# Retention attention into a routed mixture of experts on one core: token rows renumbered by step, row and sequence, and the first two experts' weights loaded in halves instead of quarters

## The chip, the cores and the metric

One core of a Trainium2 chip runs the whole program. The metric is the device time of one execution in microseconds (us). It was taken in 3 runs of the kernel before: 432.28, 426.81 and 423.11 us, with a median of 426.81 us. A separate execution was recorded by the hardware profiler; every statement about where time goes comes from that one.

## The reference

The computation has two parts. The first is a decayed linear attention over 4 sequences of 768 tokens with 8 heads of 64; its output is 3072 tokens of 512 features. The second sends each token to one of 4 groups by the largest of four logits, then to one of 4 experts in the group in the same way, and computes that expert's two-layer network.

```python
state = gamma[None, :, None, None] * state + np.einsum('bhd,bhe->bhde', k[:, :, t], v[:, :, t])
y[:, :, t] = scale * np.einsum('bhd,bhde->bhe', q[:, :, t], state)
...
x = np.ascontiguousarray(attn_out.transpose(0, 2, 1, 3)).reshape(B * S, H * D)
...
h = np.maximum(xg[mask_e] @ w1[g, e], 0.0)
ye = h @ w2[g, e]
combined = g_w[mask_g][mask_e] * e_w[mask_e]
out[tok_idx] = combined[:, None] * ye
```

So there are 16 experts, each with w1 of 512x1024 and w2 of 1024x512 in 32-bit floats (2 MB each).

## The kernel before

**Attention stage.** The tokens are cut into chunks of 128. A step handles the same chunk of two sequences, so there are 12 steps (`NS2`): steps 0 to 5 for sequences 0 and 1, steps 6 to 11 for sequences 2 and 3. In `attention`, each step `i` computes masked scores (L227, masked on VectorE at L239), the product with the running state (L278), the product with the values (L291), the new state (L253), the routing logits (L310) and, for the step before it, the transpose of the attention result to one row per token (`trans_mm`, L322 and L326). ScalarE copies these rows to the tile `xr` (L329), which has one buffer, and SyncE writes them to the DRAM tensor `xd` (L332). Each step gives 256 rows of 512 floats.

**Loads beside it.** SyncE issues all transfers of this stage from one queue in program order: q, k and v of coming steps (`load`, L177), transposed keys for two steps (`kk`, L204), the write of `xd` and the weights of the first two experts. These two, `ua` (expert 0) and `va` (expert 1), are known in advance, so their weights are fetched during attention by `wload_part` (L604). An expert's weights are four tiles `wf` of 128x2048 floats (two of w1, two of w2). Steps 2 to 9 load two parts of `ua` each; steps 9, 10 and 11 load parts of `va` by the table `NEXT`; the last tile of `va` follows after step 11. Each SyncE transfer uses one of eight completion semaphores in turn, so its issue waits for the transfer eight places before it in the queue.

**Splitting weights.** A 32-bit weight is used as a 16-bit high part `wh` (ScalarE, L616) and a 16-bit rest `wl` (L618). For `ua` GpSimd computes `wl` in pieces of 128x512, at the steps after the load; for `va` VectorE computes it in pieces of 128x1024.

**Routing and lists.** Every second step, `route` finds each token's expert, its slot in that expert's list and its weight, on VectorE. `enlist` (L440) then writes for each token its row number and weight to its slot of the DRAM tensor `meta`, by an indirect transfer that GpSimd issues. The row numbers come from the tiles `src`, filled by `iota` (L142) during setup. After 12 chunks the lists of experts 0 and 1 so far are read back to the tiles `mt` (`listed`, L630), and `gather` (L640, GpSimd, indirect) fetches these tokens' rows of `xd` into `xg`. The second lists of both experts, `ub` and `vb`, are read and gathered after all 24 chunks.

**Expert stage.** TensorE transposes gathered rows (`tpx`, L658), computes the first layer (`hps`, L681) and the second (`yps`, L713, L732, L759, L761), and GpSimd writes each result row to its place in `out` by an indirect transfer (L814). Experts 2 to 15 follow in an order found by list length, with weights in transfers of 1 MB (L590). `general` handles whatever is left in long lists, a loop that usually runs no turn.

**Order.** `manual_schedule` holds each engine to the order in which the code is written; the helper functions `beside`, `extra` and `early` inside `run` put the weight work into the steps.

Of the kernel before, what the change touches and what calls it, by code (L numbers as in the profile page):

```python
# [21 lines left out]
B, H, S, D = 4, 8, 768, 64  # L22
P = 128
NC = S // P
NCH = B * NC
NT = B * S
DM = H * D
# [66 lines left out]


KX = (4, 6)
NEXT = {9: (0, 4), 10: (4, 8), 11: (8, 12)}
KEYED = (9, 10)


class Kernel:
# [13 lines left out]
    def setup(self):  # L115
        nc, cp = self.nc, self.cp
        self.ones = cp.tile([P, P], BF16, name="ones")
        nc.vector.memset(self.ones, 1.0)
        self.cst = cst = cp.tile([P, C_END], F32, name="cst")
        self.load("q", 0, (0,))  # L120
        self.load("k", 0, (0,))
        nc.sync.dma_start(cst, self.a_cst)
        act = cp.tile([P, 1], F32, name="act")
        nc.scalar.activation(act, self.ones[:, 0:1], AF.Copy)
        self.ident = cp.tile([P, P], F32, name="ident")
        make_identity(nc, self.ident)

        self.sh = [self.pp.tile([P, 512], F32, name=f"sh{i}", tag="big", bufs=3) for i in range(3)]
        self.sh.append(self.pp.tile([P, 512], F32, name="sh3", tag="tra", bufs=1))
        for sh in self.sh:  # L130
            nc.vector.memset(sh, 0.0)
        self.wr = cp.tile([P, 4, 32], F32, name="wr")
        nc.vector.memset(self.wr, 0.0)
        self.gx = cp.tile([P, NC, 4, P], F32, name="gx")
        self.stri = cp.tile([P, P], BF16, name="stri")
        nc.vector.tensor_copy(self.stri, cst[:, C_STRI:C_STRI + P])
        self.src = []
        for i, (c0, n) in enumerate(BATCHES):
            self.src.append(cp.tile([P, BM, 2], I32, name=f"src{i}"))
            g, c = divmod(c0 // 2, NC)  # L140
            o = self.src[i][:, :, 0].rearrange("p (c b) -> p c b", b=2)
            nc.gpsimd.iota(o, pattern=[[P, n // 2], [S, 2]], base=2 * g * S + c * P, channel_multiplier=1)  # L142
        self.oh = cp.tile([P, BM + 1, NX], BF16, name="oh")
        nc.vector.memset(self.oh[:, BM, :], 0.0)
        self.base = cst[:, C_SEG:C_SEG + NX]
        warm = self.pp.tile([P, 512], F32, name="warm", tag="log", bufs=1)
        one = self.one = nc.const_aps.tensor(1.0, [P, 512], BF16)
        for i in range(WARM):
            nc.tensor.matmul(warm, one[:, 0:P], one, start=True, stop=True)
        self.log = self.pp.tile([P, 512], F32, name="log", tag="log", bufs=1)  # L150
        n = NP * CAP * 2 // P
        self.fill = cp.tile([P, n // 5], I32, name="fill")
        nc.gpsimd.memset(self.fill, OOB)
        self.meta = self.dp.tile([NP, CAP, 2], I32, name="meta")
        self.metaf = self.meta.rearrange("e r c -> (e r) c")
        self.xd = self.dp.tile([NT, DM], F32, name="xd")
# [160 lines left out]
    def trans_mm(self, i):  # L317

        nc, s = self.nc, self.st[i]
        for u in range(2):  # L320
            for j in range(4):
                nc.tensor.transpose(self.sh[2 + u][:, j * P:j * P + P], s["xt"][:, j, u], self.ident)  # L322
        for u in range(2):
            a = LG + 20 * (i % 2 * 2 + u)
            lg = self.log[:, a:a + 20]
            nc.tensor.matmul(lg, s["ls"][:, u * P:u * P + P], self.cst[:, C_SEL:C_SEL + 20], start=True, stop=True)  # L326
        xr = self.wp.tile([P, 2, DM], F32, name="xr", bufs=1)
        for u in range(2):
            nc.scalar.activation(xr[:, u], self.sh[2 + u], AF.Copy)  # L329
        g, c = divmod(i, NC)  # L330
        xd = self.xd.rearrange("(b r) f -> r b f", r=S)[c * P:c * P + P, 2 * g:2 * g + 2, :]
        nc.sync.dma_start(xd, xr)  # L332


    def route(self, i):
# [259 lines left out]

    def wload_part(self, u, k):

        i, h = divmod(k, 4)
        if k == 0:
            u["wf"], u["wh"], u["wl"] = [None] * 4, [None] * 4, [None] * 4  # L600
        if h == 0:
            u["wf"][i] = self.wst.tile([P, 2048], F32, name="wf", tag="wf", bufs=4)
        cs = slice(h * 512, h * 512 + 512)
        self.nc.sync.dma_start(u["wf"][i][:, cs], (self.a_w1, self.a_w2)[i // 2][u["e"], i % 2][:, cs])  # L604

    def wsplit(self, u, k, n=8, eng=None, high=True, low=True):
# [365 lines left out]
    def run(self):  # L972
        tc, nc = self.tc, self.nc
        with ExitStack() as ctx:
# [29 lines left out]
            def early(i, k, high):  # L1004
                if 0 <= i - 3 < 8:
                    self.wsplit(ua, 2 * i - 6 + k, 16, nc.gpsimd, high=high, low=not high)
# [8 lines left out]
            def beside(i, place):  # L1015

                last = i == NS2 - 1
                if place == -1 and i == 10:
                    self.gather(ua)
                    self.gather(va)  # L1020
                if i == 9 and place == 1:
                    assert self.done >= EARLY
                    self.listed(ua, "early0")
                    self.listed(va, "early1")
                if place == 0:
                    if 2 <= i <= 9:
                        for k in range(2):
                            self.wload_part(ua, 2 * i - 4 + k)
                    for k in range(*NEXT.get(i, (0,))):
                        self.wload_part(va, k)  # L1030
                    if i == 10:
                        self.wsplit(va, 0, low=False)
                        self.wsplit(va, 1, low=False)
                    if last:
                        self.wsplit(va, 0, high=False)
                if place == 2:
                    if last:
                        self.xtrans(ua, 'big', (0,))
                        self.wsplit(va, 2, low=False)
                if place == 1:  # L1040
                    early(i - 1, 0, False)
                    if last:
                        self.wsplit(va, 3, low=False)

            self.wp = pool("wp", 2)
            with ExitStack() as actx:
                apool = lambda name, bufs: actx.enter_context(tc.tile_pool(name=name, bufs=bufs))
                self.lp, self.vp = apool("lp", 1), apool("vp", 1)
                self.attention(extra, beside)
# [9 lines left out]
                self.wsplit(va, k, high=False)  # L1059
            first(2)  # L1060
            self.trans_mm(last)
            for k in range(12, 16):
                self.wload_part(va, k)
            while self.todo:
                self.enlist(*self.todo.pop(0))
# [136 lines left out]
```

## Time and profile before

| What | Value |
|---|---|
| median of 3 runs | 426.81 us |
| profiled execution, its own time | 427.34 us |
| its span, first to last instruction | 425.6 us |
| TensorE (PE) busy | 404.0 us, 95% |
| VectorE (DVE) busy | 290.1 us, 68% |
| ScalarE (ACT) busy | 222.8 us, 52% |
| GpSimd (POOL) busy | 175.9 us, 41% |
| mean granted TensorE clock | 0.992 |
| moved by the 16 DMA engines | 107.94 MB, mean 254 GB/s |

The profile lists instructions by engine, source line, and tile (`out<-in`). PE is the matrix product, PEld the loading of its weights. SP is SyncE; SPq and POOLq are the queues on which these engines issue transfers. A duration is in us unless it says ns; in square brackets behind an instruction stands how long its engine was idle before it and what it was released by. A stretch table gives per stretch the span's window, then each engine's busy time, the granted clock, the busy share of the 16 DMA engines and the rate in GB/s. A wait table gives who waited for whom, total time, number of times and the longest time.

### The profile page before, as it was taken

The page shows a single profiled execution, that of the slowest core. Times are in us where ns is not written, and L with a number is a line of the kernel's source. Part 1 is how long each engine was busy: PE and PEld are TensorE (multiplying, and loading weights), DVE is VectorE, ACT ScalarE, POOL GpSimd, SP SyncE. Part 2 cuts the span into 40 slices and gives each one's busy share as a digit, 9 for nine tenths or more (in the row PEclk, how much of TensorE's full clock was granted, in tenths as well). Part 3 has the DMA queues.
Part 4 walks back from the last instruction along what each step waited for, and adds up shares of the span by engine and source line. Part 5 has one row for each costly group of instructions (what it writes and reads, how often), then busy time and mean ns, then how long its engine had stood idle before and what let it go on. Part 6 is the DMA issues. An engine that isn't in the chain of part 4 may idle for free.

```text
span 425.6 us, 13495 instructions
## 1 busy us (share of the span) xinstructions
PE 404.0 (95%) x5692; PEld 332.4 (78%) x5721; DVE 290.1 (68%) x473; ACT 222.8 (52%) x342; POOL 175.9 (41%) x153
## 2 busy tenths in 40 slices
PE   8899999999798999999999999999999999999991
PEld 4789888787675768585979788897978878879791
DVE  4455585578892557776889786867768777787620
ACT  2135336446541556646556665665766657667520
POOL 4445669748877022340508142351513405222001
PEclk9999999999999999999999999999999999999996
DMA  8999999997536867776776786978788797896001
GB/s 282 378 313 327 373 306 339 336 285 243 161 94 236 333 220 249 245 258 235 257 246 214 259 277 239 315 246 283 266 286 284 272 306 270 280 327 233 27 9 34
DMA packets 36913, 107.94 MB, mean 254 GB/s; under 512 B 13784, under 2 KB 13784, under 8 KB 29684
## 3 DMA queue, kind: packets, MB, share of 16 engines
q1 hardware_dynamic: 25908, 89.76, 61.9%
q0 software_dynamic: 10944, 17.31, 11.7%
q8 instruction: 45, 0.74, 0.7%
q14 instruction: 16, 0.13, 0.1%
HBM read 94.65 MB, written 13.77 MB: 255 GB/s over the span
## 4 chain that ended last, share of the span: by engine, by line
PE 58%; issue 26%; POOL 6%; DMA 4%; DVE 2%; SPq 1%; ACT 0%; POOLq 0%; DVEq 0%; ACTq 0%
PE hps L681 19%; PE yps L713 8%; PE yps L759 6%; PE yps L761 5%; PE op L291 5%; POOL out L814 4%; PE sh L227 3%; POOL xg L640 2%; PE op L278 2%; DMA gx<-dec 2%; PE sh L322 2%; PE tpx L658 2%; PE stp L253 2%; PE sh L310 2%; PE sh L212 1%
## 5 line engine op out<-in xcount | busy, mean ns | idle before, releaser
L618 DVE TENSOR_TENSOR wl<-wf,wh 128x1024 bf16<-128x1024 f32 x120 | 148.5, 1248 | 40.0 <-ACT wh L616 35.4
L681 PE MATMUL hps<-xbh,wh 128*128 128x128 f16 (+14 forms) x576 | 134.2, 245 | 0.9 <-ACT xr L329 0.9
L681 PE MATMUL hps<-xbl,wh 128*128 128x128 bf16 (+14 forms) x576 | 134.2, 245 | 0.3 <-issue 0.3
L616 ACT ACTIVATE wh<-wf 128x1024 f16<-128x1024 f32 (+1 forms) x136 | 133.5, 1002 | 1.8 <-DMA wf<-w1p 1.8
L681 PE MATMUL hps<-xbh,wl 128*128 128x128 f16 (+14 forms) x576 | 134.2, 245 | 0.1
L814 POOL DMA_INDIRECT out<-yo,mt x32 | 41.3, 1289 | 180.4 <-ACT yo L796 152.7
L681 PEld LDWEIGHTS <-wh 128*128 128x128 f16 x1152 | 102.5, 98 | 4.7 <-issue 1.9
L640 POOL DMA_INDIRECT xg<-xd,mt x32 | 52.5, 1641 | 26.3 <-DMA mt<-meta 17.4
L686 ACT ACTIVATE hh<-hps 128x256 f16<-128x256 f32 (+14 forms) x72 | 35.1, 488 | 52.3 <-PE hps L681 51.5
L761 PEld LDWEIGHTS <-wh 128*128 128x128 f16 x704 | 44.7, 98 | 21.0
L681 PEld LDWEIGHTS <-wl 128*128 128x128 bf16 x576 | 56.3, 98 | 1.1 <-issue 0.5
L239 DVE TENSOR_TENSOR pf<-sh,cst 128x512 f32<-128x512 f32 x48 | 30.8, 685 | 30.0 <-PE sh L227 10.3
L689 DVE SCALAR_TENSOR_TENSOR hl<-hps,hh 128x256 bf16<-128x256 f32 (+14 forms) x69 | 38.1, 553 | 16.7 <-ACT hh L686 14.2
L660 ACT ACTIVATE xbh<-tpx 128x512 f16<-128x512 f32 (+13 forms) x32 | 16.9, 527 | 47.2 <-PE tpx L658 47.1
L661 DVE TENSOR_TENSOR xbl<-tpx,xbh 128x512 bf16<-128x512 f32 (+13 forms) x32 | 19.2, 601 | 21.5 <-ACT xbh L660 21.5
L440 POOL DMA_INDIRECT meta<-src,slot x24 | 27.6, 1151 | 14.3 <-DVE src L394 7.1
L759 PE MATMUL yps<-wh,hh 128*128 128x512 f16 x88 | 33.4, 380 | 0.0
L759 PE MATMUL yps<-wh,hl 128*128 128x512 f16 x88 | 33.4, 379 | 0.0
L187 POOL TENSOR_TENSOR vs<-lv,cst 128x512 f32<-128x512 f32 x24 | 24.6, 1047 | 20.8 <-DMA lv<-qkv 10.9
L761 PEld LDWEIGHTS <-wl 128*128 128x128 bf16 x352 | 23.1, 98 | 10.4
L761 PE MATMUL yps<-hh,wl 128*128 128x103 f16 (+10 forms) x352 | 26.3, 197 | 1.2
L761 PE MATMUL yps<-hl,wh 128*128 128x103 bf16 (+10 forms) x352 | 26.3, 197 | 0.0
(146 smaller groups left out, 600.0 us busy)
## 6 DMA issues: line engine op xcount, KB each, us to landing
wf<-w1p SPq DMA_DIRECT2D x26, 1024.0 KB
wf<-w2p SPq DMA_DIRECT2D x26, 1024.0 KB
xd<-xr SPq DMA_DIRECT2D x12, 512.0 KB
lq<-qkv SPq DMA_DIRECT2D x11, 512.0 KB
lk<-qkv SPq DMA_DIRECT2D x11, 512.0 KB
lv<-qkv SPq DMA_DIRECT2D x11, 512.0 KB
wf<-w1p SPq DMA_DIRECT2D x16, 256.0 KB
wf<-w2p SPq DMA_DIRECT2D x16, 256.0 KB
```

The costliest lines, as they stand in the source:

```text
L239: nc.vector.tensor_tensor(o, sc, tri, ALU.mult)
L440: i = nc.gpsimd.indirect_dma_start(out=self.metaf, out_offset=bass.IndirectOffsetOnAxis(ap=slot[:, c:c + 1], axis=0), in_=src[:, c, :], in ...
L616: nc.scalar.activation(u["wh"][i][:, cs], u["wf"][i][:, cs], AF.Copy)
L618: (eng or nc.vector).tensor_tensor(u["wl"][i][:, cs], u["wf"][i][:, cs], u["wh"][i][:, cs], ALU.subtract)
L640: nc.gpsimd.indirect_dma_start(out=xg[0:r, i, :], out_offset=None, in_=self.xd[0:n, :], in_offset=bass.IndirectOffsetOnAxis(ap=mt[0:r, i, ...
L681: nc.tensor.matmul(hv[:, a, 0:W], l[:, k, fs], r[:, k, 0:W], start=(n == 0), stop=(n == 11))
L686: nc.scalar.activation(hh[:, f, 0:W], hv[:, :, 0:W], AF.Relu)
L689: nc.vector.scalar_tensor_tensor(*rest)
L713: nc.tensor.matmul(ps[0:r, :], l[:, k, ts], m[k], start=(n == 0), stop=(n == 23))
L759: nc.tensor.matmul(big, h[:, k, 0:P], w[k], start=(n == 0), stop=(n == 23))
L761: nc.tensor.matmul(yv[:, d, 0:r], w[k][:, d * P:d * P + P], h[:, k, P:P + r], start=(n == 0 and d == 0), stop=(n == 23), skip_group_check= ...
L814: s = nc.gpsimd.indirect_dma_start(out=self.out, out_offset=bass.IndirectOffsetOnAxis(ap=mt[0:r, i, 0:1].bitcast(U32), axis=0), in_=yo[0:r ...
```

## The change

Three edits, all of them about the size and place of transfers.

1. **Row numbers.** Before, the row of a token in `xd`, in the lists and in `out` is its sequence number times 768 plus its position. Now it is 256 times the step, plus twice the row in the chunk, plus which of the two sequences it is. `iota` writes the new numbers; `trans_mm` writes `xr` as one piece of 1024 floats per partition, where it wrote two pieces of 512; the host puts the rows of `out` back into the reference's order after the run.
2. **Weight parts.** `wload_part` loads halves of a tile (128x1024 floats, 512 KB) instead of quarters (128x512, 256 KB). There are 16 such transfers in place of 32.
3. **Their places.** Steps 2 to 9 issue one half where they issued two quarters; `NEXT` and the last load are renumbered so that the same bytes go out at the same places.

```diff
-NEXT = {9: (0, 4), 10: (4, 8), 11: (8, 12)}
+NEXT = {9: (0, 2), 10: (2, 4), 11: (4, 6)}
...
-            g, c = divmod(c0 // 2, NC)
             o = self.src[i][:, :, 0].rearrange("p (c b) -> p c b", b=2)
-            nc.gpsimd.iota(o, pattern=[[P, n // 2], [S, 2]], base=2 * g * S + c * P, channel_multiplier=1)
+            nc.gpsimd.iota(o, pattern=[[2 * P, n // 2], [1, 2]], base=c0 * P, channel_multiplier=2)
...
-        g, c = divmod(i, NC)
-        xd = self.xd.rearrange("(b r) f -> r b f", r=S)[c * P:c * P + P, 2 * g:2 * g + 2, :]
-        nc.sync.dma_start(xd, xr)
+        xd = self.xd[2 * P * i:2 * P * i + 2 * P, :].rearrange("(p u) f -> p (u f)", u=2)
+        nc.sync.dma_start(xd, xr.rearrange("p u f -> p (u f)"))
...
-        i, h = divmod(k, 4)
+        i, h = divmod(k, 2)
...
-        cs = slice(h * 512, h * 512 + 512)
+        cs = slice(h * 1024, h * 1024 + 1024)
...
                     if 2 <= i <= 9:
-                        for k in range(2):
-                            self.wload_part(ua, 2 * i - 4 + k)
+                        self.wload_part(ua, i - 2)
...
-            for k in range(12, 16):
+            for k in (6, 7):
                 self.wload_part(va, k)
...
-    return r.results[0]["out"]
+    out = r.results[0]["out"].reshape(B // 2, NC, P, 2, DM)
+    return np.ascontiguousarray(out.transpose(0, 3, 1, 2, 4)).reshape(NT, DM)
```

No engine's instructions change their order. On SyncE the queue gets shorter. The first place is one step in the middle of attention (steps 2 and 3); the rows are SyncE's issues, a row being the line, the tile written and the tile read with its shape. Before:

```order
L332 DMA xd<-xr 128x2x512
L604 DMA wf<-w1p 128x512 x2
L177 DMA lq<-qkv 128x1024
L177 DMA lv<-qkv 128x1024
L177 DMA lk<-qkv 128x1024
```

Now:

```order
L330 DMA xd<-xr 128x1024
L602 DMA wf<-w1p 128x1024
L176 DMA lq<-qkv 128x1024
L176 DMA lv<-qkv 128x1024
L176 DMA lk<-qkv 128x1024
```

A step's six issues become five, in the same order. The second place is steps 8 to 10, where the first lists (`mt`) are read back. Before:

```order
L204 DMA kk<-kt 128x1024
L332 DMA xd<-xr 128x2x512
L604 DMA wf<-w2p 128x512 x2
L604 DMA wf<-w1p 128x512 x4
L630 DMA mt<-meta 128x2 x2
L204 DMA kk<-kt 128x1024
L332 DMA xd<-xr 128x2x512
L604 DMA wf<-w1p 128x512 x4
```

Now:

```order
L203 DMA kk<-kt 128x1024
L330 DMA xd<-xr 128x1024
L602 DMA wf<-w2p 128x1024
L602 DMA wf<-w1p 128x1024 x2
L628 DMA mt<-meta 128x2 x2
L203 DMA kk<-kt 128x1024
L330 DMA xd<-xr 128x1024
L602 DMA wf<-w1p 128x1024 x2
```

The lists stand behind three weight transfers where they stood behind six; the bytes ahead of them are the same.

## The prediction

> **What bounds the kernel now.** I read the page's shares first, then the stretches, then who waits.
>
> ```profile
> span 425.6 us, 13495 instructions
> PE 404.0 (95%) x5692; PEld 332.4 (78%) x5721; DVE 290.1 (68%) x473; ACT 222.8 (52%) x342; POOL 175.9 (41%) x153
> 0.00:135.00 135.00, 124.43 (x2385) 102.69 (x2388) 87.90 (x223) 54.19 (x106) 87.88 (x94) 1.00 0.83 279
> 135.00:404.00 269.00, 267.10 (x3082) 217.69 (x3108) 198.95 (x245) 165.66 (x229) 85.19 (x57) 1.00 0.75 259
> 404.00:425.60 21.60, 12.44 (x230) 12.01 (x227) 3.27 (x6) 2.92 (x7) 2.84 (x3) 0.84 0.07 25
> ```
>
> PE is the bound. Its idle time is 10.6 us up to 135 (first column after the length of the stretch), 1.9 us from there to 404, and 9.2 us in the tail. The change touches transfers between 26 and 121 us alone, so it can win only what PE waits before 135; a byte moved faster under a busy PE is worth nothing. These waits, from 18 to 106 us and from 100 to 140 us (the first lines of each):
>
> ```profile
> PE sh L227 <- issue: 0.8, 1, 0.8
> PE op L278 <- DVE slot L419: 0.5, 1, 0.5
> PE log L326 <- ACT ls L315: 0.4, 2, 0.2
> ...
> PE tpx L658 <- DMA xg<-xd,mt: 1.6, 1, 1.6
> PE log L399 <- DVE oh L374: 1.3, 1, 1.3
> PE sh L310 <- ACT xr L329: 1.0, 1, 1.0
> PE hps L681 <- ACT xr L329: 0.9, 1, 0.9
> ```
>
> Not one wait in the attention steps names a transfer. The four at the end of routing, 4.8 us together, are all that faster transfers could reach. They hang on this chain: lists read back, gather, GpSimd's queue, last lists, last gather.
>
> ```profile
> 85.57 3.14 SPq L604 DMA_DIRECT2D wf<-w1p  x4
> 88.81 1.01 SPq L630 DMA_DIRECT2D mt<-meta  x2
> ...
> 96.17 1.08 POOL L640 DMA_INDIRECT xg<-xd,mt  x1 [6.63 <-DMA mt<-meta]
> 98.62 2.05 POOL L187 TENSOR_TENSOR vs<-lv,cst 128x512 f32<-128x512 f32 x2
> ...
> 107.64 2.28 POOL L618 TENSOR_TENSOR wl<-wf,wh 128x512 bf16<-128x512 f32 x2
> ...
> 117.83 0.97 POOL L1054 MEMSET xg<- 128x1024 f32 x1
> 118.97 1.00 POOL L440 DMA_INDIRECT meta<-src,slot  x1 [0.17 <-DVE hl L1081]
> ...
> 129.08 1.05 POOL L640 DMA_INDIRECT xg<-xd,mt  x1 [2.88 <-DMA mt<-meta]
> ...
> 132.53 0.66 PE L658 MATMUL tpx<-ident,xg 128*128 128x128 f32 x4 [1.58 <-DMA xg<-xd,mt]
> ```
>
> GpSimd sits 6.63 us until the first lists have landed at 96.17 and then works nearly without a gap until 118.80; the last four list writes start at 118.97; from them come the second lists, the gather at 129.08 and the matrix product at 132.53, for which PE idled 1.58 us.
>
> **The change part by part.** *Issues.* Sixteen transfers vanish from SP. Four quarters took 3.14 us to issue (85.57), that is 0.79 us each, so two take about 1.6 us and the lists go out some 1.6 us earlier than 88.81. The same megabyte is still ahead of them on the same engines, so by itself this is worth 0: their cover is the queue of data, and without that queue it would be 1.6 us on GpSimd's chain. Elsewhere in the stage the saved issue time lies under SP's own waits:
>
> ```profile
> SPq L332 <- ACT xr L329: 24.5, 9, 5.6
> SPq L177 <- PE sh L212: 15.5, 6, 3.5
> ```
>
> The `xd` write comes first in each group and waits for ScalarE, the loads wait for PE to free their tiles; neither moves.
>
> *Pieces.* The 12 `xd` writes go from 3072 pieces of 2048 bytes to 1536 of 4096, the weight parts from 4096 to 2048: 3584 fewer. What a piece costs is not shown directly, so I bound it by three stretches (their engine rows; the packets, MB and share of SP's queue from 86 to 90; two issues):
>
> ```profile
> 10.00:20.00 10.00, 8.75 (x230) 7.42 (x228) 5.01 (x9) 1.74 (x3) 4.48 (x5) 1.00 1.01 383
> 42.00:50.00 8.00, 7.18 (x177) 6.05 (x173) 5.59 (x17) 2.40 (x6) 4.21 (x5) 1.00 1.01 386
> 86.00:90.00 4.00, 4.00 (x82) 3.38 (x77) 2.32 (x7) 0.83 (x3) 3.55 (x4) 1.00 0.91 173
> q1 hardware_dynamic: 378, 0.69, 90.5%
> ...
> 42.30 0.38 SPq L332 DMA_DIRECT2D xd<-xr  x1
> 42.73 1.55 SPq L604 DMA_DIRECT2D wf<-w1p  x2
> ```
>
> From 10 to 20 nearly all data comes in 4096-byte pieces, at 383 GB/s with the engines full (the last two columns). From 42 to 50 one `xd` write and two quarters, 1 of the 3 MB, go in 2048-byte pieces, and the rate is 386. By this end the piece size costs nothing and the gain is 0. From 86 to 90, with the quarters of `va` in flight, the engines are 0.91 busy at only 173 GB/s: 4 us x 16 x 0.905 / 378 = 153 ns a packet of 1.8 KB. If that time belongs to the packet and not to its bytes, double pieces save half the stretch, 2 us, and the lists land 2 us earlier. The full-rate stretch is the nearer row for most of the stage, the slow one for just the transfers ahead of the lists, so I take a third of it: lists 0.7 us earlier. A loss is not excluded either: a half must land whole before its first piece is split, at most 0.68 us more (256 KB at 386 GB/s). GpSimd and ScalarE split `ua` one step after the load, so only `va`'s splits could feel it.
>
> [...]
>
> *What 0.7 us at the lists is worth.* The gather, and GpSimd behind it, move up 0.7 us, until VectorE becomes late: `src` of the last batch is ready at 118.40, GpSimd is free at 118.80.
>
> ```profile
> 118.22 0.18 DVE L394 RECIPROCAL src<-log 128x4 f32<-128x4 f32 x1
> 108.68 4.61 DVE L618 TENSOR_TENSOR wl<-wf,wh 128x1024 bf16<-128x1024 f32 x3
> L618 DVE TENSOR_TENSOR wl<-wf,wh 128x1024 bf16<-128x1024 f32 x120 | 148.5, 1248 | 40.0 <-ACT wh L616 35.4
> ```
>
> So 0.4 us count (118.80 - 118.40). VectorE itself: three splits took 4.61 us where three at the mean of 1248 ns take 3.74, a loss of 0.87 us while GpSimd ran its own splits (107.64 to 109.92). GpSimd's splits and VectorE's lie on each other for 1.24 us (108.68 to 109.92); 0.7 us less of that would be worth 0.5 of the 0.87, but GpSimd's next list writes move into the place, so I count 0.2 us. Together 0.6 us, which PE's wait of 1.58 us can take in full.
>
> *Row numbers.* `iota` keeps its six instructions in setup; the list writes, gathers and result writes keep their number and 2048-byte rows. From 135 on PE idles 1.9 us in 269, so a gather or result write would have to be late by many microseconds to show; I cost this at 0, and its cover is the double buffer of gathered rows.
>
> *Sum.* Issues 0, pieces and chain -0.6, row numbers 0: the profiled execution's 427.34 us (span 425.6 and 1.74 around it) becomes 426.7. It stands 0.53 above the median of the runs, so the forecast on the median's scale is **426.2 us**.
>
> **The rivals.** *Packets have a fixed time.* If the slow stretches are set per piece, the lists land 2 us or more earlier, VectorE gets its whole 0.87 us back beside the 0.4, and the waits of PE on `xr` shrink since the `xd` write ends sooner. For it: the 173 GB/s. Against: 386 GB/s with a third of the bytes in small pieces. The gain is 1.3 us by the chain, and at most all four waits, 4.8 us; I put it at 2.5: 424.3 us.
>
> *Slower: the write of `xd` takes longer.* `xr` has one buffer.
>
> ```profile
> 107.32 6.43 SPq L332 DMA_DIRECT2D xd<-xr  x2
> 112.27 1.08 ACT L329 ACTIVATE xr<-sh 128x512 f32<-128x512 f32 x2 [2.41 <-DMA xd<-xr]
> 114.15 0.24 ACT L362 ACTIVATE ex<-log 128x80 f32<-128x80 f32 x1 [0.80 <-DVE log L360]
> ```
>
> Step 10's write is issued at 107.32 and releases ScalarE at 112.27, 4.95 us later, after 2.41 us of waiting. ScalarE then has 0.80 us to spare before the exponential of the last routing batch. A write that takes over 0.8 us longer delays this, the last list writes, the gather and PE, one for one. Half as long again would be 2.5 us, less 0.8: +1.7, so 428.5 us. For it: the rate falls to 173 GB/s in a stretch a few us behind an `xd` issue. Against: fewer, larger, adjoining pieces have no reason in any row to be slower.
>
> *The change does not do what it says:* the engines still cut at 2048 bytes, only 16 issues go, and the time stays 426.8 us. Against it:
>
> ```profile
> DMA packets 36913, 107.94 MB, mean 254 GB/s; under 512 B 13784, under 2 KB 13784, under 8 KB 29684
> q1 hardware_dynamic: 25908, 89.76, 61.9%
> ```
>
> 36913 - 29684 = 7229 packets are 8 KB or more, and 56 whole tiles of 128 rows of 8192 bytes are 7168: a row goes as one packet.
>
> **How the numbers follow.** My forecast has 0.64, the fixed packet time 0.16, the slower write 0.11, no effect 0.09. All four lie within 2% (8.5 us), which is about what a measurement of this kernel can tell from no change; PE's waits before 135 cannot give 8.5 us, and a loss of that size needs a write of some 14 us. What is left for the outer cases is the spread of the runs, 423.11 to 432.28: I give 0.03 to each side and 0.94 to no change. The mechanisms reach from 422.0 (426.8 - 4.8) to 428.5; with the runs' spread on top the range is 421.5 to 430.
>
> **What would show it.** Right: SP's queue (q1) has 3600 to 3900 packets less than 25908; PE busy stays near 404 us; PE's wait before the transposes of the second gather is about 1.0 instead of 1.58 us; the first gather starts near 95.5 and the last list writes near 118.6. The rival with fixed packet time would show in a rate well over 173 GB/s ahead of the lists, and a first gather at 94 or earlier. The slower write would show in ScalarE's wait before `xr` above 3.2 us. I am wrong if PE's busy time in the expert stage moves, if a gather comes late there, or if the first gather starts after 97.

## The result and the profile after

The changed kernel takes 429.17 us (median of 22 runs, 425.24 to 436.07), the kernel before 426.93 (22 runs, 423.11 to 432.28). The ratio is 1.0055, with a 95% interval of 1.0032 to 1.0079: a loss of some 2.3 us, where 0.6 us of gain was forecast. The profiled execution after has 429.85 us (span 428.2), 2.51 more than before's 427.34. The profiles of three experiments below (e1, e11, e18) fell in disturbed executions; their rows are not read.

The line numbers of after are lower by one to three (the gather's L640 is L638 here). The page of after, its span, busy times, packets and SP's queue:

```profile
span 428.2 us, 13486 instructions
PE 404.0 (94%) x5721; PEld 332.1 (78%) x5721; DVE 288.9 (67%) x473; ACT 223.6 (52%) x342; POOL 177.7 (42%) x153
DMA packets 33073, 107.94 MB, mean 252 GB/s; under 512 B 13528, under 2 KB 13528, under 8 KB 25844
q1 hardware_dynamic: 22068, 89.76, 62.2%
```

SP's queue has 25908 - 22068 = 3840 packets less, the 3584 that were counted and 256 of under 512 bytes (13784 - 13528), 16 for each of the 16 issues saved. So the change does what it says. But the packets' time is no less: 62.2% of 428.2 us is 266 us an engine, 61.9% of 425.6 was 263. The work is the same too, 404.0 us of PE; it is PE's idle time that grew. The stretches of after, cut where the same work begins and ends:

```profile
0.00:136.50 136.50, 121.60 (x2381) 101.77 (x2382) 86.62 (x223) 55.01 (x106) 89.62 (x94) 0.99 0.84 276
136.50:405.50 269.00, 268.99 (x3102) 217.43 (x3101) 198.06 (x245) 165.67 (x229) 85.25 (x57) 1.00 0.76 259
405.50:428.20 22.70, 13.38 (x242) 12.95 (x240) 4.22 (x7) 2.92 (x7) 2.84 (x3) 0.84 0.09 32
```

Before 136.5 us PE idles 14.9 us, where it idled 10.6 before 135. The rows of PE's waits from 18 to 140 us:

```profile
PE tpx L656 <- DMA xg<-xd,mt: 2.8, 1, 2.8
PE op L277 <- DVE xt L302: 1.7, 2, 1.5
PE stp L252 <- DMA kk<-kt: 1.5, 1, 1.5
PE op L277 <- DVE pf L238: 1.3, 1, 1.3
```

Two of the four largest name a transfer, one of them in the attention steps, where none did before. The chain that was to move up did not. SP in after:

```profile
84.93 1.34 SPq L602 DMA_DIRECT2D wf<-w1p  x2
89.22 0.96 SPq L628 DMA_DIRECT2D mt<-meta  x2
90.29 2.34 SPq L203 DMA_DIRECT2D kk<-kt  x1
```

The weight issues are done at 86.27, 2.4 us before those of the kernel before (88.71), yet the lists go out at 89.22 instead of 88.81. SP's wait there, from 88 to 95 us:

```profile
SPq L628 <- DMA meta<-src,slot: 2.9, 1, 2.9
```

The read of the lists needs their last write on GpSimd's queue to have landed; before, the weight issues lay over that wait. The write itself was issued at 83.88 us, where it was issued at 83.16 before. GpSimd in after, the first gather, the last batch of list writes and the second gather:

```profile
96.48 1.08 POOL L638 DMA_INDIRECT xg<-xd,mt  x1 [6.22 <-DMA mt<-meta]
...
119.28 1.00 POOL L438 DMA_INDIRECT meta<-src,slot  x1 [0.17 <-DVE hl L1078]
...
123.29 3.04 POOL L438 DMA_INDIRECT meta<-src,slot  x1 [0.30 <-DVE ord L488]
...
130.55 1.04 POOL L638 DMA_INDIRECT xg<-xd,mt  x1 [2.37 <-DMA mt<-meta]
```

96.17 became 96.48, 118.97 became 119.28, 129.08 became 130.55. The last list write, 3.04 us here, was shorter before:

```profile
122.98 1.93 POOL L440 DMA_INDIRECT meta<-src,slot  x1 [0.30 <-DVE ord L490]
```

So of the 1.47 us at the second gather 0.31 stood at the first one already, and 1.11 came in that write. And PE:

```profile
93.70 0.99 PE L277 MATMUL op<-lq,V 64*64 64x128 f32 x27 [1.28 <-DVE pf L238]
98.83 1.15 PE L252 MATMUL stp<-vs,kk 128*64 128x64 f32 x32 [1.47 <-DMA kk<-kt]
134.08 1.07 PE L656 MATMUL tpx<-ident,xg 128*128 128x128 f32 x4 [2.82 <-DMA xg<-xd,mt]
```

These rows look like an explanation: lists late, keys late, gather late. The experiments show that two single profiles do not carry it.

### The profile page after: what moved, and what is told of

Same layout as the page of the kernel before. It is cut to its first block, busy times and chain, and to the rows that moved or that the text cites. A ratio compares the mean times of both kernels' runs of the same rounds, so it can differ in the third digit from the quotient of the medians.

```text
span 428.2 us, 13486 instructions
## 1 busy us (share of the span) xinstructions
PE 404.0 (94%) x5721; PEld 332.1 (78%) x5721; DVE 288.9 (67%) x473; ACT 223.6 (52%) x342; POOL 177.7 (42%) x153
## 2 busy tenths in 40 slices
DMA packets 33073, 107.94 MB, mean 252 GB/s; under 512 B 13528, under 2 KB 13528, under 8 KB 25844
## 3 DMA queue, kind: packets, MB, share of 16 engines
q1 hardware_dynamic: 22068, 89.76, 62.2%
HBM read 94.65 MB, written 13.77 MB: 253 GB/s over the span
## 4 chain that ended last, share of the span: by engine, by line
PE 56%; issue 23%; DMA 8%; POOL 7%; DVE 4%; SPq 1%; POOLq 0%; ACT 0%; DVEq 0%; ACTq 0%
PE hps L679 19%; PE yps L711 8%; PE yps L757 6%; PE yps L759 5%; PE op L290 4%; POOL out L812 3%; PE sh L226 3%; POOL xg L638 2%; DMA gx<-dec 2%; DMA meta<-src,slot 2%; PE tpx L656 2%; PE sh L321 2%; PE op L277 2%; PE stp L252 2%; DMA wf<-w1p 1%
## 5 line engine op out<-in xcount | busy, mean ns | idle before, releaser
L638 POOL DMA_INDIRECT xg<-xd,mt x32 | 52.6, 1645 | 25.2 <-DMA mt<-meta 16.4
L438 POOL DMA_INDIRECT meta<-src,slot x24 | 28.7, 1198 | 14.0 <-issue 4.4
L757 PE MATMUL yps<-wl,hh 128*128 128x512 bf16 x88 | 33.4, 379 | 0.0
```

What stands on the lines that cost most here:

```text
L438: i = nc.gpsimd.indirect_dma_start(out=self.metaf, out_offset=bass.IndirectOffsetOnAxis(ap=slot[:, c:c + 1], axis=0), in_=src[:, c, :], in ...
L638: nc.gpsimd.indirect_dma_start(out=xg[0:r, i, :], out_offset=None, in_=self.xd[0:n, :], in_offset=bass.IndirectOffsetOnAxis(ap=mt[0:r, i, ...
L757: nc.tensor.matmul(big, h[:, k, 0:P], w[k], start=(n == 0), stop=(n == 23))
```

## The experiments

Each ratio is to the kernel before, in runs taken with it on the same chip, with its 95% interval. There were four chips: one for e1 to e4, a second for e5 to e8, a third for e9 to e12, a fourth for e13 to e18. Experiments taken together share their runs of the kernel before, so their ratios are not independent. The diffs are against the kernel before unless another is named.

**e1_halves: the weight halves alone.**

```diff
-NEXT = {9: (0, 4), 10: (4, 8), 11: (8, 12)}
+NEXT = {9: (0, 2), 10: (2, 4), 11: (4, 6)}
...
-        i, h = divmod(k, 4)
+        i, h = divmod(k, 2)
...
-        cs = slice(h * 512, h * 512 + 512)
+        cs = slice(h * 1024, h * 1024 + 1024)
...
-                        for k in range(2):
-                            self.wload_part(ua, 2 * i - 4 + k)
+                        self.wload_part(ua, i - 2)
...
-            for k in range(12, 16):
+            for k in (6, 7):
```

> Only the weight parts are changed (halves of 512 KB, 16 transfers for 32); row numbers and the write of xd are as before. Theory A (the halves make the loss: SyncE no longer waits in its ring of eight, so more weight bytes stand ahead of the transposed keys and the lists): the whole loss is here, ratio 1.004 to 1.008, about 2.3 us, and TensorE waits for the transposed keys again (1.5 us in the changed kernel). Theory B (the write of xd in 4096-byte pieces makes it): ratio 0.998 to 1.002.

Measured: 1.0010 (0.9968 to 1.0053). It tells nothing by itself; e7 repeats it.

**e2_rows: the rows of x alone**, the numbers in the lists and the order of the result with them.

```diff
-        xd = self.xd.rearrange("(b r) f -> r b f", r=S)[c * P:c * P + P, 2 * g:2 * g + 2, :]
-        nc.sync.dma_start(xd, xr)
+        xd = self.xd[2 * P * i:2 * P * i + 2 * P, :].rearrange("(p u) f -> p (u f)", u=2)
+        nc.sync.dma_start(xd, xr.rearrange("p u f -> p (u f)"))
```

> Only the row numbers and the write of xd are changed; the weights still load in quarters of 256 KB. Theory A: ratio 0.998 to 1.002. Theory B: ratio 1.004 to 1.008, with longer packets at the times of the xd writes. If both ratios come out at 1.002 to 1.004, the loss is shared and belongs to larger pieces as such.

Measured: 0.9979 (0.9945 to 1.0012). The write of x does not make the loss.

**e3_again: the changed kernel, unchanged.** No diff to it.

> The changed kernel once more, beside the others on the same chip. All theories: ratio 1.003 to 1.008. For the trace: the theory that the drop of TensorE's clock is set by its wait before the second gather expects a half-clock stretch of about 3.4 us whenever that wait is over about 2.5 us, and none when it is near 1.6 us.

Measured: 1.0025 (0.9984 to 1.0066): the two intervals of the change overlap, and the loss may be nearer 0.4% than 0.55%. PE's wait before the second gather's transposes is 1.87 us in its profile, and no half clock follows it; one stands at 110.97 us instead, where 1.66 of the 3.41 us before were idle.

**e4_warm: the changed kernel with eight matmuls ahead of the second gather's transposes.** They write a bank that the transposes overwrite.

```diff
+            for _ in range(heat):
+                nc.tensor.matmul(tp, self.ones, self.one, start=True, stop=True)
...
-                    self.xtrans(ub, "sta")
+                    self.xtrans(ub, "sta", heat=8)
```

> The changed kernel with eight matrix products of 512 columns, whose result is overwritten, put on TensorE ahead of the transposes of the second gather. They run in the wait and keep the engine busy for some 1.7 us of it. Theory C (a good part of the loss is the half clock behind the wait, 1.7 us each time it comes): ratio against before 1.000 to 1.003, and no half-clock stretch behind 134 us. If the loss is only waiting: 1.004 to 1.008 as in the changed kernel.

Measured: 1.0112 (1.0041 to 1.0183). PE in its profile, from 135.5 us:

```profile
136.21 1.90 PE L656 MATMUL tpx<-const-bfloat16-1.0,ones 128*128 128x512 bf16 x8
138.11 0.66 PE L658 MATMUL tpx<-ident,xg 128*128 128x128 f32 x4
```

The ratio lies above both numbers expected. Here PE came to the place only at 136.21, straight from other work; there was no gap to fill, and the 1.90 us stood on the path. That is half of the 3.7 us by which the ratio lies above e3's, and the interval is wide. The half clock behind the gather, 134.16 to 137.58 us in after's profile, is not there, but another such stretch is, at 112.97. No gain from the full clock at this place shows; what the half clock costs elsewhere is an estimate (last section).

**e5_before: the kernel before, against itself.** No diff.

> The kernel before, unchanged, timed against itself: a second profile of it, and a test of how far the comparison strays by itself. In all five profiles of kernels with an edit TensorE stands 1.3 to 2.7 us in step 9 after a few of the scores' matmuls, always at the same place of the program, and 0.45 us there in the one profile of before; the profile names a different VectorE result each time, but the stall always ends 1.24 to 1.47 us after a 16384-byte packet of the queue 'q8 instruction' has landed. Theory F (the edit makes TensorE's code arrive later): here again under 0.7 us at that place, and a ratio of 1.000 within 0.003. Theory S (the stall and the half-clock windows come and go from run to run, and before's one profile was a lucky one): 1 to 2.7 us here too, the ratio still 1.000.

Measured: 0.9989 (0.9959 to 1.0020). Its profile has a span of 429.8 us, 4.2 more than the first of the same kernel. PE in it, the longest stops without a transfer:

```profile
70.86 0.56 PE L227 MATMUL sh<-lq,lk 64*64 64x128 f32 x14 [1.59 <-issue]
...
97.27 1.57 PE L278 MATMUL op<-lq,V 64*64 64x128 f32 x27 [2.02 <-DVE log L387]
```

The second stop is in step 10, in its product with the running state (the expectation counts it as step 9 and as the scores). At this place, where the first profile of before showed 0.45 us and after 1.28, before itself shows 2.02. Theory S holds and F falls: this stop comes and goes in every version. So do the half-clock stretches (none in before's first profile, two here before 140 us). The chain of lists and gathers strays as well, here in before:

```profile
92.31 1.08 SPq L630 DMA_DIRECT2D mt<-meta  x2
99.79 1.08 POOL L640 DMA_INDIRECT xg<-xd,mt  x1 [7.53 <-DMA mt<-meta]
```

The lists went out 3.09 us later than in after and the first gather started 3.31 us later, in another execution of the kernel before. What differed most between the two profiles is not what differs between the kernels; only many runs tell.

**e6_cut: quarters of 64 partitions by 1024 columns.**

```diff
-        cs = slice(h * 512, h * 512 + 512)
-        self.nc.sync.dma_start(u["wf"][i][:, cs], (self.a_w1, self.a_w2)[i // 2][u["e"], i % 2][:, cs])
+        ps = slice(h % 2 * 64, h % 2 * 64 + 64)
+        cs = slice(h // 2 * 1024, h // 2 * 1024 + 1024)
+        self.nc.sync.dma_start(u["wf"][i][ps, cs], (self.a_w1, self.a_w2)[i // 2][u["e"], i % 2][ps, cs])
```

> The kernel before with its weight quarters cut the other way: 64 partitions by 1024 columns instead of 128 by 512, so the packets are of 4096 bytes, as in the changed kernel, while the pieces stay 256 KB, their number stays 32, and the rows of x are untouched. Theory P (the larger packet itself costs: what shares an engine with it, code and lists, waits longer behind each): as slow as the changed kernel, 1.004 to 1.006. Theory R (the size and number of pieces: the ring of eight issues no longer holds SP back, so more bytes stand in front of what SP issues next): 1.000 within 0.002. Theory S: 1.000 too; R and S part at the next run.

Measured: 1.0157 (1.0112 to 1.0203), three times what theory P gives. SP's queue in its page, and below it that of e7 (packets of the same size on all partitions):

```profile
q1 hardware_dynamic: 23860, 89.76, 63.9%
```

```profile
q1 hardware_dynamic: 23604, 89.76, 61.8%
```

63.9% of 431.5 us is 276 us an engine, 61.8% of 429.8 is 266. The same bytes took 10 us more an engine, on the mean, when half the partitions took them at a time. That is a cost of this cut, not of the packet's size, so the run leaves P open.

**e7_halves: e1 once more.** The diff is e1's.

> The 512 KB halves alone once more, in more rounds (its first time, 1.001 with 0.9968 to 1.0053, could not be told from either): the rows of x as before. Theories P and R (the halves make the loss): 1.004 to 1.006, an interval that leaves out 1.000. If the loss needs both parts of the change, or is none of the halves': 1.000 within 0.002.

Measured: 1.0065 (1.0026 to 1.0104). The halves make the loss.

**e8_noload: without the 32 weight pieces of the two first experts.** It leaves out their output.

```diff
-        if h == 0:
-            u["wf"][i] = self.wst.tile([P, 2048], F32, name="wf", tag="wf", bufs=4)
-        cs = slice(h * 512, h * 512 + 512)
-        self.nc.sync.dma_start(u["wf"][i][:, cs], (self.a_w1, self.a_w2)[i // 2][u["e"], i % 2][:, cs])
+        if getattr(self, "blank", None) is None:
+            self.blank = self.wst.tile([P, 2048], F32, name="wf", tag="wf", bufs=4)
+            self.nc.vector.memset(self.blank, 0.0)
+        if k == 0:
+            u["wf"], u["wh"], u["wl"] = [self.blank] * 4, [None] * 4, [None] * 4
```

> The kernel before without the 32 weight pieces of the two first experts: their tiles are one tile of zeros, so those two experts' output is left out of the computation, while all instructions of the engines stay. It takes 8 MB off the queue of steps 2 to 11. Theory F (TensorE's code waits behind the weight packets): the stalls that end 1.2 to 1.5 us after a code packet, 0.15, 0.32 and 0.45 us in before's profile and up to 2.7 us in the others, are gone or under 0.2 us each, the steps 3 to 10 take 8.0 us each where they took 8.1 to 9.4, and the whole is 3 to 6 us shorter. If code arrives late for another reason, those stalls stay, and the gain is what the steps' other waits for transfers were, under 2 us.

Measured: 0.9940 (0.9906 to 0.9973), 2.6 us less. PE in its profile, at two places where it stopped in before:

```profile
78.17 0.69 PE L253 MATMUL stp<-vs,kk 128*64 128x64 f32 x16 [0.97 <-issue]
...
91.22 0.45 PE L278 MATMUL op<-lq,V 64*64 64x128 f32 x4 [0.42 <-issue]
91.95 0.77 PE L278 MATMUL op<-lq,V 64*64 64x128 f32 x18 [0.29 <-issue]
```

The stop of step 10 between the second and the third of these matmuls is gone; two smaller ones, 0.42 and 0.29 us, stand some matmuls further on. The other place, 0.15 us in the first profile of before, has 0.97 us here. Eight megabytes of weights are worth 2.6 us in all, about as much as the change lost by cutting them differently. The expectation of theory F, 3 to 6 us, is missed, and so is the other, under 2 us.

**e9_strided: 512 KB pieces of 2048-byte packets.** Against e1:

```diff
-        cs = slice(h * 1024, h * 1024 + 1024)
-        self.nc.sync.dma_start(u["wf"][i][:, cs], (self.a_w1, self.a_w2)[i // 2][u["e"], i % 2][:, cs])
+        o, w = u["wf"][i], (self.a_w1, self.a_w2)[i // 2][u["e"], i % 2]
+        o, w = (t.rearrange("p (a b f) -> p a b f", a=2, b=2)[:, :, h, :] for t in (o, w))
+        self.nc.sync.dma_start(o, w)
...
+        if n == 16:
+            h = (0, 2, 1, 3)[h]
```

> The halves alone, but each 512 KB piece is made of two column blocks of 512 that do not touch, so that its packets stay 2048 bytes as in the kernel before; ScalarE converts the quarters in the order in which they come. Number and size of the pieces as in the changed kernel, packets as before, rows of x as before. Theory P (the 4096-byte packet makes the loss): 1.000 within 0.002, as before. Theory R (the pieces: half as many issues, the ring of eight no longer holds SP back, more bytes in flight): 1.004 to 1.006, as the halves alone (1.001 and 1.0065 in their two calls).

Measured: 1.0060 (1.0027 to 1.0094). SP's queue in its page:

```profile
q1 hardware_dynamic: 25652, 89.76, 62.2%
```

25652 - 23604 = 2048: the halves' 2048 packets of 4096 bytes have become 4096 of 2048, and the loss stays.

**e10_strided_rows: the same with the rows of x.** The diff is e9's, against the changed kernel.

> The whole change, its weight pieces cut in the same way, so that only the write of x has 4096-byte packets. Theory P: 0.998 to 1.000, like the rows of x alone (0.9979). Theory R: 1.004 to 1.006, like the changed kernel.

Measured: 1.0054 (1.0013 to 1.0095). Theory P falls twice: the loss comes with the 512 KB piece, whatever its packets. One thing more differs in e9 and e10: a split of the second expert's weights (1024 columns) now needs two pieces to have landed, where it needed one in e1. e11, which loads these weights in quarters, is free of that.

**e11_ua: halves for the first expert only.**

```diff
+        n = 2 if u["tag"] == "a" else 4
-        i, h = divmod(k, 4)
+        i, h = divmod(k, n)
...
-        cs = slice(h * 512, h * 512 + 512)
+        w = 2048 // n
+        cs = slice(h * w, h * w + w)
...
+            ua["tag"], va["tag"] = "a", "b"
...
-                        for k in range(2):
-                            self.wload_part(ua, 2 * i - 4 + k)
+                        self.wload_part(ua, i - 2)
```

> The 512 KB halves for the first expert only (one piece in each of steps 2 to 9); the second expert's weights, which load in steps 9 to 11 and behind them, stay in quarters; rows of x as before. If the loss comes from the steps 2 to 9, where SP's queue is fullest (a 96% share of the DMA engines from 16 to 94 us): 1.004 to 1.006. If it comes from the four large pieces in front of the second load of transposed keys and of the lists (steps 9 to 11): 1.000 within 0.002.

Measured: 1.0056 (1.0017 to 1.0095). One piece instead of two in each of steps 2 to 9 is enough; the four large pieces ahead of the lists and the keys are not needed for the loss.

**e12_rows: e2 once more.** The diff is e2's.

> The rows of x alone once more, weights in quarters as before: the candidate for the fastest version. If the larger write pieces are worth something, 0.996 to 0.999 again and an interval below 1.000 together with the first time (0.9979); if they are worth nothing, 1.000 within 0.002.

Measured: 1.0013 (0.9978 to 1.0048). With e2's 0.9979 the rows of x are worth nothing that can be measured.

**e13_uneven: each half as two pieces of 896 and 128 columns.** Against e1:

```diff
-        cs = slice(h * 1024, h * 1024 + 1024)
-        self.nc.sync.dma_start(u["wf"][i][:, cs], (self.a_w1, self.a_w2)[i // 2][u["e"], i % 2][:, cs])
+        ends = (0, 896, 1024)
+        for a, b in zip(ends, ends[1:]):
+            cs = slice(h * 1024 + a, h * 1024 + b)
+            self.nc.sync.dma_start(u["wf"][i][:, cs], (self.a_w1, self.a_w2)[i // 2][u["e"], i % 2][:, cs])
```

> The 512 KB halves, each cut in two unequal pieces of 896 and 128 columns (448 KB and 64 KB): as many issues as in the kernel before (32), nearly all bytes in pieces nearly as large as in the changed one; rows of x as before. Theory I (the number of issues: SP's ring of eight fills as before and holds the later loads back): 1.000 within 0.002. Theory L (the size of the single piece): 1.004 to 1.006.

Measured: 1.0013 (0.9978 to 1.0048). From here on the runs are of the fourth chip, on which neither the change nor e1 was run; what this leaves open stands behind the table.

**e14_uneven2: the small piece first.** Against e13:

```diff
-        ends = (0, 896, 1024)
+        ends = (0, 128, 1024)
```

> The same with the small piece (128 columns) issued ahead of the large one: a second sample of the same question, in which only the order inside a pair differs. Theory I: 1.000 within 0.002. Theory L: 1.004 to 1.006.

Measured: 1.0003 (0.9966 to 1.0039). Both samples lie at 1: on this chip pieces of 448 KB cost nothing that shows when there are as many issues as before. That is theory I's number and not that of L, the size of the single piece.

**e15_eighths: the first expert's weights in 128 KB pieces.** Against e11:

```diff
-        n = 2 if u["tag"] == "a" else 4
+        n = 8 if u["tag"] == "a" else 4
...
-                        self.wload_part(ua, i - 2)
+                        for k in range(4):
+                            self.wload_part(ua, 4 * i - 8 + k)
```

> The other direction: the first expert's weights in pieces of 128 KB (four in each of steps 2 to 9, twice as many as before), the second expert's in quarters and the rows of x as before. Theory L, if smaller is always better: 0.995 to 0.998. Theory I: 0.995 to 0.998 too, or, if the issues themselves begin to cost (0.42 us each, two more a step, on a queue that waits some 16 us in all between 18 and 94 us), 1.000 to 1.004. A result of 1.004 or more means that 256 KB was the best of the three sizes and that SP's issues have a price as well.

Measured: 1.0017 (0.9980 to 1.0054). Neither theory's gain shows: more issues than two a step bring nothing more.

**e16_behind: e1 with the first expert's piece behind the loads of q and v.**

```diff
-                    if 2 <= i <= 9:
-                        self.wload_part(ua, i - 2)
...
                 if place == 2:
+                    if 2 <= i <= 9:
+                        self.wload_part(ua, i - 2)
```

> The halves, with the first expert's piece of each step issued behind the loads of q and v of three steps on instead of ahead of them; rows of x as before. Theory Q (the loss is that the large piece stands whole in front of q, v and k, whose landing the steps wait for): 0.998 to 1.001. If the place in the queue does not matter: 1.004 to 1.006, as the halves in their old place.

Measured: 1.0008 (0.9975 to 1.0042). With the single piece behind q and v no loss shows either, though there are as few issues as in the change: theory Q's number came too, so I is not the whole of it. SP's issues in one step each in e7 (loss), e13 and e16 (no loss), each in its own profile:

```profile
52.30 0.38 SPq L332 DMA_DIRECT2D xd<-xr  x1
52.73 0.46 SPq L604 DMA_DIRECT2D wf<-w1p  x1
53.61 0.40 SPq L177 DMA_DIRECT2D lq<-qkv  x1
```

```profile
49.81 0.38 SPq L332 DMA_DIRECT2D xd<-xr  x1
50.24 1.43 SPq L606 DMA_DIRECT2D wf<-w1p  x2
51.76 1.09 SPq L177 DMA_DIRECT2D lq<-qkv  x1
52.95 0.38 SPq L177 DMA_DIRECT2D lv<-qkv  x1
```

```profile
50.62 0.38 SPq L332 DMA_DIRECT2D xd<-xr  x1
51.31 0.33 SPq L177 DMA_DIRECT2D lq<-qkv  x1
52.81 0.33 SPq L177 DMA_DIRECT2D lv<-qkv  x1
53.19 0.49 SPq L604 DMA_DIRECT2D wf<-w1p  x1
```

In e7 the load of q follows the write of x by 1.31 us with one weight piece between them; in e13 by 1.95 us with two issues; in e16 by 0.69 us, with the weights behind it. So it is not just when q goes out.

**e17_qbehind: quarters in that later place.**

```diff
-                    if 2 <= i <= 9:
-                        for k in range(2):
-                            self.wload_part(ua, 2 * i - 4 + k)
...
                 if place == 2:
+                    if 2 <= i <= 9:
+                        for k in range(2):
+                            self.wload_part(ua, 2 * i - 4 + k)
```

> The kernel before with only the place changed: the first expert's two quarters of each step are issued behind the loads of q and v of three steps on; quarters and rows as before. The halves in that place came out level with before (1.0008), where in the old place they cost half a per cent. If the place takes away what the large piece costs: 1.000 within 0.002 here, the place being worth nothing by itself. If the place is a gain of its own that only makes up for the loss (theory L still standing): 0.994 to 0.997.

Measured: 0.9997 (0.9965 to 1.0030). The place is worth nothing that shows by itself, so it does not just pay for a loss in e16.

**e18_whole_uneven: the whole change, each half as 896 and 128 columns.** The diff is e13's, against the changed kernel.

> The whole change, rows of x too, with each 512 KB piece issued as two unequal ones (896 and 128 columns), so that the number of issues is that of the kernel before. Theory I: 0.998 to 1.001, the loss of the change gone. If the two samples without the rows (1.0013 and 1.0003) were luck: 1.004 to 1.006, like the change.

Measured: 0.9969 (0.9937 to 1.0001). With sixteen further issues the whole change shows no loss; against the kernel before it cannot be told from no difference.

All runs side by side, by how the first expert's weights go out:

| weights of a step | ratios | mean |
|---|---|---|
| one 512 KB piece, ahead of q and v (the change, e1, e3, e7, e9, e10, e11) | 1.0055 1.0010 1.0025 1.0065 1.0060 1.0054 1.0056 | 1.0046 |
| two or more pieces, or the piece behind q and v (e2, e5, e12 to e18) | 0.9979 0.9989 1.0013 1.0013 1.0003 1.0017 1.0008 0.9997 0.9969 | 0.9999 |

e4, e6 and e8 change other things and stand apart. The halves make a loss, and those of the first expert are enough: on the third chip 1.0054 to 1.0060 stand against e12's 1.0013, on the second e7's 1.0065 against e5's 0.9989; on the first, 1.0010 and 1.0025 are not clear of 1. What takes the loss away is less sure. Of the second row, all runs in which the weights go out in another form or place than before (e13 to e18) are of the fourth chip. No single piece ahead of q and v was measured there, and whether this chip would show the loss at all is not known. For it speaks that the kernel before took as long there as on the others (medians of 429.50 and 429.12 us, against 428.90 to 429.73). Against it speaks that PE's stop in step 10 (last section) is in ten of the other twelve profiles and in none of the five of this chip, whatever the pieces. Runs of e1 there would decide it.

## Why the prediction was wrong

The time, 429.17 us, lies inside the range of 421.5 to 430.0 and inside the 2% that I gave 0.94; the sign is wrong. That it lies inside owes to the spread of the runs, which the range takes in, and not to the mechanism; that the rival of the slower write, 428.5, came nearest is luck too. Step by step:

*Issues, costed at 0.* **This is the step that failed.** I wrote that the issues saved are worth nothing by themselves and that elsewhere they lie under SP's own waits, so that "neither moves". In place of 0, weight pieces issued once instead of twice cost 0.46% on the mean, some 2.0 us. I had asked only whether a removed issue could win time. Shown is that the single large piece in each of steps 2 to 9 is enough for the loss (e11). So it is not the loss that I did weigh, a half that must land whole before its first split: I charged that to `va` alone, and e11 loads `va` in quarters. That the loss takes both the smaller number of issues (not two pieces, e13, e14 and e18) and the place ahead of q and v (e16) is argued from the fourth chip and not shown.

Which wait carries the loss stays open. The sum of PE's waits from 18 to 150 us is 7.6, 9.5, 10.2 and 8.7 us in four profiles with quarters (before, e5, e2, e12) and 11.9, 8.8, 11.0, 9.6 and 9.9 in five with single pieces (after, e3, e7, e9, e10): means 9.0 and 10.2, with overlap, and no one place holds the difference. In the five of the fourth chip it is 7.2 to 10.9, with a mean of 9.4. That q, v or the lists land later was argued and is not shown: SP's wait for the list writes, 2.9 us in after, is 3.1, 4.4 and 3.8 us in e13, e16 and e17, which show no loss. Nor does the ring of eight show: SP's waits for a weight transfer, from 18 to 94 us, are 2.1 us in the first profile of before and 1.2 in e2, but there are none in e5, e12, e13 and e14, which have as many issues.

*Pieces, -0.6 us.* There was no such gain. Larger packets did not shorten the transfers (266 us an engine, against 263 and 267 in the two profiles of before), and changing the packet alone changed nothing (e9 against e7 and e11, e2 and e12 against 1). By the trace of before, a packet of 2048 bytes on SP's queue takes 84 ns at the median, one of 4096 bytes 159 and one of 8192 bytes 309, so here the time goes with the bytes. The third of the slow stretch that I took should have been the other bound, 0, given by the row at 386 GB/s.

*Lists 0.7 us earlier.* They went out 0.41 us later. The wait for the list writes to land (2.9 us) was hidden under the weight issues; I named the queue of data as cover for the saved issues and did not see this second one. The last list writes then started at 119.28, not 118.6. VectorE's part came out larger than the 0.2 us that I counted: its three splits took 3.76 us instead of 4.61 (three at the mean take 3.74), yet no time came of it.

```profile
109.84 3.76 DVE L616 TENSOR_TENSOR wl<-wf,wh 128x1024 bf16<-128x1024 f32 x3
112.92 1.09 ACT L328 ACTIVATE xr<-sh 128x512 f32<-128x512 f32 x2 [1.90 <-DMA xd<-xr]
```

*"Not one wait in the attention steps names a transfer."* True of that profile and too weak a ground. A profile shows one run: the same kernel, profiled again, had stops of 1.59 and 2.02 us in those steps (e5).

*Row numbers, 0.* Right: from 136.5 us on PE idles 0.01 us in 269.

*The rivals.* Fixed packet time: refuted (e9, e10); the first gather started at 96.48, not at 94 or earlier. The slower write of x: refuted; ScalarE's wait before `xr` is 1.90 us instead of 2.41 (second row above), and the rows alone are level. No effect: refuted by the 3840 packets. The case that came, a loss from the weights' larger pieces, was none of the three.

## What to carry to other kernels

SP had time to spare here (its waits between 18 and 94 us sum to 41 us in the first profile of before), and merging its weight issues still came with a loss of half a per cent (1.0046 on the mean of seven ratios). Try the new piece size with the old number of issues and in another place of the queue, and run the plain change beside them on the same chip: without it a loss that is gone may never have been there. Before explaining a difference of half a per cent from two profiles, profile the old kernel a second time; here it differed from itself by 4.2 us of span, in the very waits that looked like the cause.

## What the runs showed of the hardware

**Half a clock came in stretches of 3.413 us.** The clock record of after has one ahead of the tail, from 134.16 us on, 3.413 us long. In e9 three of them start at 41.69, 96.30 and 113.37 us; the first and the last are 71.68 us apart, which is 21 times 3.413, and the middle one starts 16 such lengths behind the first. The stretch ahead of the half one and the half one itself, in after (the last three numbers of a row are clock, DMA share and GB/s):

```profile
130.75:134.16 3.41, 0.59 (x4) 0.10 (x3) 0.00 (x0) 0.00 (x0) 3.05 (x4) 1.00 0.49 100
134.16:137.58 3.42, 3.42 (x11) 1.68 (x12) 0.69 (x1) 0.60 (x1) 2.86 (x4) 0.50 1.01 350
```

and in e5:

```profile
94.12:97.53 3.41, 1.39 (x47) 1.12 (x47) 3.17 (x13) 1.00 (x2) 0.00 (x0) 1.00 1.04 369
97.53:100.94 3.41, 3.41 (x68) 3.27 (x62) 0.30 (x2) 2.11 (x2) 1.08 (x1) 0.50 1.01 356
```

Each row has PE's busy time behind its length: 2.82 and 2.02 us of idle time in one stretch, and the next is at half clock. By my estimate that costs a busy PE some 1.7 us more (half of 3.41). With the profiles read here cut into such stretches, from 12 to 150 us, all seven stretches with 2.0 us or more of idle time were followed by a half one (after; e5; e12; e15 twice; e16; e17); between 1.3 and 2.0 us some were (1.41 us in e9) and some were not (1.85 us in e7). In e4 a stop of 2.65 us lay across the edge of two stretches, 1.83 us of the second were idle, and no half clock followed. I read this as the same wait costing 1.7 us more or not by where it falls; one such case does not show it. The half clock does not set the kernels apart: 0, 2, 1 and 2 such stretches in the four profiles with quarters, 1, 2, 1, 3 and 0 in the five with single pieces.

**A stop of PE ended behind a packet of the queue `instruction`.** The page of after lists this queue:

```profile
q8 instruction: 45, 0.74, 0.7%
```

That is 0.74 MB in 45 packets, 16 KB each. In ten of the seventeen profiles read here PE stops in step 10, between the second and the third matmul of the product with the running state. The stop is put down to one VectorE result or another, but in each of the ten it ended 1.21 to 1.47 us after a packet of this queue had landed (landing and resumption in us by the trace's records, and the stop):

| | before | after | e2 | e3 | e4 | e5 | e7 | e9 | e10 | e12 |
|---|---|---|---|---|---|---|---|---|---|---|
| landed | 91.64 | 92.32 | 93.58 | 94.31 | 96.29 | 95.95 | 94.65 | 95.58 | 94.13 | 93.91 |
| PE goes on | 93.05 | 93.70 | 95.05 | 95.55 | 97.73 | 97.27 | 96.00 | 96.79 | 95.39 | 95.33 |
| stop | 0.45 | 1.28 | 1.81 | 1.28 | 2.65 | 2.02 | 1.95 | 2.02 | 1.54 | 1.68 |

In these ten, PE began the product at most 0.58 us after the landing, in nine of them before it. In the seven without the stop (e6, e8, e13 to e17) the last packet had landed 1.10 to 4.18 us before PE began. So what the ten have in common is the packet and not the named result; that PE waited for the packet is my inference from these times and not shown. The stop does not make the loss: e2, e5 and e12 have it and are level (0.9979, 0.9989 and 1.0013). Without the weight loads the packet came 4.18 us ahead (e8), but it came ahead in e13 to e17 too, which load them; what sets its time is open.

**Writes to half the partitions took longer here.** Cutting the same bytes by partitions (e6) took 276 us an engine, on the mean of the 16 DMA engines, where e7's cut took 266, and the time of the kernel was 1.57% longer than before's.
